# Another order of filter loads and of the first products in a Fourier-mixing and SwiGLU kernel

## The chip, the core and the metric

The kernel runs on one core of a Trainium2 chip. The metric is the time of one execution on the device, in microseconds (us). The core has five engines that run side by side, each through its own list of instructions in order: TensorE (PE) multiplies matrices, VectorE (DVE) and ScalarE (ACT) work element by element and copy results out of PSUM, GpSimd (POOL) works element by element and also starts DMA transfers, and SyncE (SP) only starts transfers. An instruction that waits holds up all that stand behind it on its engine.

## What is computed

The reference takes `x` of shape (8, 3008, 256) and complex filters of shape (1505, 256), given as a real and an imaginary array. It does

```
X = rfft(x, axis=1)
y = irfft(X * (filt_r + i filt_i), n=3008, axis=1)
x2 = y.reshape(24064, 256)
xn = x2 / sqrt(mean(x2^2) + 1e-6) * rms_g
out = (silu(xn @ w_gate) * (xn @ w_val)) @ w_out
```

with `w_gate` and `w_val` of shape (256, 1536) and `w_out` of shape (1536, 256). The output is float32.

## The kernel before

The transform of length 3008 = 64 * 47 is done in two stages of matrix products, with twiddle factors folded into tables. For one batch: stage A multiplies by a 64-point table; a transposition brings the other index onto the partitions; stage B multiplies by a 47-point table for each of 32 indices k (`b_mm`, line 228, two values of k make one unit, so there are 16 units); the result is multiplied by the real and by the imaginary filter (`b_unit`, line 244, the two products L268 and L269); then come the inverse of stage B (`bi_unit`, or `bit_unit` at line 562 for batch 0), another transposition and the inverse of stage A. Then the feed-forward part (`gv`, line 432, and `down`, line 451) goes over 48 blocks of rows, and its products fill PE. The work of batches 1 to 7 is laid out in numbered slots between the blocks of the feed-forward loop; batch 0 has no such loop to lie in, and it comes first, with an order written out by hand (lines 655 to 783). The change touches this part only.

**Batch 0.** `x_load` (line 179) brings the input in four chunks of two transfers each through POOL's queue. `at_unit` (line 525) does stage A. `t1_mm(g)` (line 537) transposes eight 128x128 blocks on PE into PSUM, for four values of k; PSUM has two buffers each for even and odd g. `t1_copy(g, on_act)` (line 555) copies the result out, on ACT (L558) or on DVE (L560). Unit i of stage B needs the copy of g = i // 2. The products of unit i are done by DVE, but for units 3, 7, 9 and 12: there ACT first copies the stage-B result (`v`, L266), and POOL does the two products from that. `inverses` runs `bit_unit` for units of `i`; ACT copies its results (`gT`, L581). `warm_up` issues products of zeros on PE that nothing reads.

**The filters.** Both filter arrays are kept in four groups of eight values of k: tiles `fr0` to `fr3` and `fi0` to `fi3`, of 128 partitions by 8 by 256 float32. `f_load(c, e, eng)` (line 503) loads group c of the real (e = 0) or imaginary (e = 1) array into one half of the partitions, through the queue of `eng`: one transfer of 24 rows of 8 KB (L506) and two of 12 rows in which the eight values of k run backwards (L509, 1 KB pieces); group 0 has a fourth (L513). `f_dup(c, e, eng, lo, hi)` (line 515) copies that half to the other half of the partitions: on ACT (L519), on POOL (L523), or as a transfer on SP's queue (L521). Group c serves units 4c to 4c + 3. Before the loads, the other halves and the gaps are set to zero on DVE (L664), ACT (L652) and POOL (L657, L658).

**The order of loads.** SP's queue carries fr0, fr1, fr2, fr3, fi3 and then the doubling of fr3. POOL's queue carries the input, then fi0, fi1, fi2. A queue's transfers are started in order, and with eight completion semaphores a queue, a transfer is started only when the one eight places before it has landed.

**`gate(ap)`** (line 624) copies one element with POOL into a small tile of its own; it waits for the data it reads, and with it all that stands behind it on POOL. The kernel before defines it and does not call it.

Of the kernel before, what the change touches and what calls it, by code (L numbers as in the profile page):

```python
# [121 lines left out]
def kernel(  # L122
# [11 lines left out]
    nc = tc.nc  # L134

    tab = {k: nc.inline_tensor(np.ascontiguousarray(v), name=k + "_t").ap()
           for k, v in _make_tables().items()}
# [38 lines left out]
    st = {b: {"x": {}, "t1": {}, "t2": {}, "s": {}, "t3": {}, "t4": {}, "y": {}, "sq": {},  # L176
              "u": {}, "xn": {}} for b in range(B)}
# [50 lines left out]
    def b_mm(b, i):  # L228
        ps = bank(3 if b else (0, 3, 4, 5)[i % 4], "psb").rearrange("p (a d) -> p a d", a=2)
        if b == 0 and i > 3:  # L230
            nc.tensor.matmul(ps[:, 0, :], wz[:, 0:P], wz[:, 0:D], start=True, stop=True)
        for u in range(2):
            k = 2 * i + u
            if b:
                w, t = late_p["wb"], st[b]["t2"][k // KC][:, k % KC, :]
            else:
                w, t = wbp, st[0]["t2"][k // 4][:, k % 4, :]
            nc.tensor.matmul(ps[:, u, :], w[:, k, :], t, start=True, stop=True)  # L238
        return ps
# [4 lines left out]
    def b_unit(b, i, ps=None):  # L244
        if ps is None:
            ps = b_mm(b, i)
        f1, f2 = filt(2 * i, 2)
        if b:
            s1 = late_p["sp"].tile([P, 2, D], FP16, tag="s1", name="s1")
            s2 = late_p["sp"].tile([P, 2, D], FP16, tag="s2", name="s2")  # L250
            if summed(b, i):
                nc.vector.tensor_tensor(out=s1, in0=ps, in1=f1, op=ALU.mult)  # L252
                st[b]["s"][i] = (s1, s2, ps, f2)
                return
        elif i % 2:
            s1 = hp.tile([P, 512], FP16, tag="sg", name="sg").rearrange("p (a d) -> p a d", a=2)
            s2 = hhs[(i // 2) % 4].rearrange("p (a d) -> p a d", a=2)
        else:
            ss = xnp.tile([P, 2, 512], FP16, tag="xn", name="ss")
            s1, s2 = (ss[:, e, :].rearrange("p (a d) -> p a d", a=2) for e in range(2))  # L260
        eng = nc.vector
        if (i in (3, 5, 8, 12, 15)) if b else (i in (3, 7, 9, 12)):
            eng = nc.gpsimd
            v = yp.tile([P, 2, 512], FP32, tag="y", name="v")
            v = v[:, 0, :].rearrange("p (a d) -> p a d", a=2)
            nc.scalar.activation(out=v, in_=ps, func=AXT.Copy)  # L266
            ps = v
        eng.tensor_tensor(out=s1, in0=ps, in1=f1, op=ALU.mult)  # L268
        eng.tensor_tensor(out=s2, in0=ps, in1=f2, op=ALU.mult)  # L269
        st[b]["s"][i] = (s1, s2)  # L270
# [229 lines left out]
    def raw(src, row, ap):  # L500
        return bass.AP(tensor=src.tensor, offset=src.offset + row * D, ap=ap)

    def f_load(c, e, eng):
        lo = 1 if c == 0 else 0
        src, t, p0 = ((filt_r, fr[c], 0), (filt_i, fi[c], HALF))[e]
        eng.dma_start(t[p0 + 16:p0 + 63:2, :, :].rearrange("p a d -> p (a d)"),  # L506
                      raw(src, c * KC, [[64 * D, 24], [1, KC * D]]))
        for g in range(2):
            eng.dma_start(t[p0 + 1 + 24 * g:p0 + 24 + 24 * g:2, lo:KC, :],  # L509
                          raw(src, 64 * (1 + 11 * g) - c * KC - lo,  # L510
                              [[64 * D, 12], [-D, KC - lo], [1, D]]))
        if c == 0:
            eng.dma_start(t[p0 + 1:p0 + 48:2, 0, :], raw(src, 32, [[64 * D, 24], [1, D]]))  # L513

    def f_dup(c, e, eng, lo=0, hi=KC):
        t = (fr, fi)[e][c][:, lo:hi, :]
        a, o = (0, HALF) if e else (HALF, 0)
        if eng is nc.scalar:
            eng.activation(out=t[a:a + HALF], in_=t[o:o + HALF], func=AXT.Copy)  # L519
        elif eng is nc.sync:  # L520
            eng.dma_start(t[a:a + HALF], t[o:o + HALF])  # L521
        else:
            eng.tensor_copy(out=t[a:a + HALF], in_=t[o:o + HALF])  # L523
# [13 lines left out]
    def t1_mm(g):  # L537
        if g < 6:
            if g % 2 == 0:
                st[0]["t2t"] = t2p.tile([KR, KC, D], FP16, tag="t2", name="t2")  # L540
            dst = st[0]["t2t"][:, 4 * (g % 2):4 * (g % 2) + 4, :]
        else:
            dst = t3p.tile([KR, 4, D], FP16, tag="t3", name="t2")
        st[0]["t2"][g] = dst
        pool, tag = ((psG, "pg"), (psV, "pv"))[g % 2]
        ps = pool.tile([P, 4, D], FP16, tag=tag, name="pt1")
        af = aT.rearrange("p a k -> p (a k)")
        for a in range(4):
            for dh in range(2):
                b0 = dh * H * P  # L550
                src = af[:, b0:b0 + 32 * P].rearrange("p (i k) -> p k i", k=K2)[:, 4 * g + a, :]
                nc.tensor.transpose(ps[:, a, ts(dh, P)], src, ident)
        st[0]["t2ps"][g] = ps

    def t1_copy(g, on_act):
        dst, ps = st[0]["t2"][g], st[0]["t2ps"].pop(g)
        if on_act:
            nc.scalar.activation(out=dst, in_=ps[0:KR], func=AXT.Copy)  # L558
        else:
            nc.vector.tensor_copy(out=dst, in_=ps[0:KR])  # L560
# [63 lines left out]
    def gate(ap):  # L624

        g = up.tile([1, 1], FP32, tag="gate", name="gate")
        nc.gpsimd.tensor_copy(out=g, in_=ap)
# [8 lines left out]
    with tc.manual_schedule():  # L636
# [28 lines left out]
            zero(fi[c][HALF:P])  # L665
        with nc.allow_non_contiguous_dma(reason="one gain a partition"):
            nc.sync.dma_start(gsb, moe_rms_g.rearrange("(a p) -> p a", p=P))
        for c in range(4):
            f_load(c, 0, nc.sync)
            f_load(c, 1, nc.gpsimd if c < 3 else nc.sync)  # L670

        warm_up(14, 1)
        for g in range(4):
# [14 lines left out]
        def products(*units):  # L688
            for i in units:
                b_unit(0, i, psb.pop(i))  # L690

        def stage_b(*units):
            for i in units:
                psb[i] = b_mm(0, i)

        def inverses(*units):
            for i in units:
                bit_unit(i)

        for g in range(4):  # L700
            t1_mm(g)
            t1_copy(g, g == 1)
        stage_b(0, 1, 2, 3)
        for g in range(4, 8):
            t1_mm(g)
        f_dup(0, 0, A, 0, 2)
        f_dup(0, 1, G, 0, 2)
        f_dup(0, 0, A, 2, 4)
        f_dup(0, 1, G, 2, 8)
        t1_copy(4, 1)  # L710
        f_dup(0, 0, G, 4, 8)
        products(0)
        stage_b(4)
        products(1)
        stage_b(5)
        t1_copy(5, 1)
        f_dup(1, 1, G)
        products(3)
        f_dup(1, 0, A, 0, 4)
        f_dup(1, 0, A, 4, 8)  # L720
        inverses(0, 1)
        products(2)
        t1_copy(6, 0)
        t1_copy(7, 0)
        stage_b(6, 7)
        f_dup(2, 1, G)
        f_dup(3, 0, S)
        products(4, 7)
# [201 lines left out]
```

## Time and profile before

| | |
|---|---|
| median of 6 runs | 886.2 us |
| lowest, highest | 885.66, 888.01 us |
| the profiled execution | 885.66 us, of which the span of the profile is 883.7 us |
| granted TensorE clock | 0.998 |
| busy: PE, DVE, ACT, POOL | 872.9, 678.0, 625.1, 437.6 us |
| first product of the feed-forward loop (L443) | at 45.01 us |
| last inverse product of batch 0 (L573) | at 37.54 us |
| last piece of fi3 copied by ACT (L519) | at 32.83 us |

How to read the rows of a timeline: start in us from the begin of the span, length of the piece in us, engine, line, operation, output<-input, partitions x elements and types, and how many instructions (x2) the row holds; in brackets, how long the engine was idle before it and what ended that. SPq is SP's list of transfers; its rows show when a transfer is started, not when it lands. In the chain of work that ended last, each row is a start, a length and what the end of the program hung on in that time. A row of stretches has start:end, the busy time of each engine with its number of instructions, the granted clock, the DMA engines' mean busy share, and GB/s.

### The profile page before, as it was taken

The numbers are of one execution on the slowest core, as the hardware profiler recorded it, in microseconds if no ns is written. First come the engines' busy times: TensorE is split into PE (matmuls) and PEld (weight loads), VectorE is DVE, ScalarE is ACT, GpSimd is POOL, SyncE is SP. The second block draws the span as 40 slices with busy tenths as digits, with TensorE's granted clock in tenths as the row PEclk, the third lists the DMA queues.
The fourth block names the chain that finished last, engine by engine and source line by source line (L and its number), as shares of the span: only waits on it lengthen the run. The fifth ranks groups of instructions, "written<-read, shape, count | busy, mean of one in ns | idle before, by whom it ended". The sixth has DMA issues, their size and how long they took to land.

```text
span 883.7 us, 17466 instructions
## 1 busy us (share of the span) xinstructions
PE 872.9 (99%) x6257; PEld 559.7 (63%) x6257; DVE 678.0 (77%) x1086; ACT 625.1 (71%) x1070; POOL 437.6 (50%) x394
## 2 busy tenths in 40 slices
PE   9899999999999999999999999999999999999997
PEld 6666666666666666666666666666666666666556
DVE  8866777898878877978687887888778887555555
ACT  8877667677677766876677766887567765676444
POOL 8834831646436752676237661376415761155300
PEclk9999999999999999999999999999999999999999
DMA  9796826665643565434735247322442233222302
GB/s 206 128 186 161 175 70 205 150 142 131 191 122 74 110 144 160 98 96 101 209 83 132 84 100 185 100 80 78 110 141 79 67 84 78 72 64 50 72 24 49
DMA packets 80095, 101.44 MB, mean 115 GB/s; under 512 B 8108, under 2 KB 56684, under 8 KB 79560
## 3 DMA queue, kind: packets, MB, share of 16 engines
q1 hardware_dynamic: 69688, 84.23, 34.5%
q0 software_dynamic: 10240, 15.96, 11.6%
q8 instruction: 49, 0.80, 0.4%
q14 instruction: 38, 0.31, 0.1%
q10 hardware_dynamic: 80, 0.13, 0.1%
HBM read 67.67 MB, written 46.78 MB: 130 GB/s over the span
## 4 chain that ended last, share of the span: by engine, by line
PE 94%; DVE 2%; DMA 2%; ACT 1%; issue 1%; ACTq 0%
PE po L462 28%; PE pg L443 27%; PE pv L443 27%; PE psi L291 3%; PE psb L238 3%; PE psn L323 2%; PE psa L203 2%; DMA fr<-in_filt_r_dram 1%; DMA fi<-in_filt_i_dram 1%; DVE fr L664 1%; PE psq L352 1%; DVE o L472 0%; PE pt L592 0%; ACT gT L581 0%; DVE wi L616 0%
## 5 line engine op out<-in xcount | busy, mean ns | idle before, releaser
L448 DVE TENSOR_TENSOR hh<-pv,sg 128x512 f16<-128x512 f32 (+2 forms) x588 | 392.7, 670 | 189.0 <-ACT sg L447 78.1
L447 ACT ACTIVATE sg<-pg 128x512 f16<-128x512 f32 (+2 forms) x588 | 340.9, 580 | 221.1 <-PE pg L443 211.0
L462 PE MATMUL po<-wo,hh 128*128 128x256 f16 x2244 | 342.2, 272 | 0.7 <-DVE hh L448 0.3
L443 PE MATMUL pv<-xn,wv 128*128 128x512 f16 (+2 forms) x1176 | 339.6, 370 | 0.0
L443 PE MATMUL pg<-xn,wg 128*128 128x512 f16 (+2 forms) x1176 | 339.6, 370 | 0.0
L462 PEld LDWEIGHTS <-hh 128*128 128x128 f16 x2256 | 216.4, 98 | 95.7 <-issue 1.5
L282 POOL TENSOR_TENSOR s<-s,s 128x512 f16<-128x512 f16 x101 | 116.6, 1155 | 223.7 <-DVE s L276 153.9
L443 PEld LDWEIGHTS <-wv 128*128 128x128 f16 x1176 | 114.8, 98 | 128.8 <-issue 0.3
L419 POOL TENSOR_TENSOR xn<-y,rb 128x1024 f16<-128x1024 f32 (+1 forms) x45 | 126.0, 2801 | 54.2 <-DMA rb<-r_tmp 53.1
L443 PEld LDWEIGHTS <-wg 128*128 128x128 f16 x1176 | 111.3, 98 | 13.3 <-issue 0.3
L358 POOL TENSOR_TENSOR rho<-u,mhalf 128x4 f32<-128x4 f32 (+1 forms) x48 | 49.0, 1020 | 61.9 <-DVE u L356 61.7
L296 ACT ACTIVATE t<-psi 96x512 f16<-96x512 f32 x112 | 66.4, 593 | 8.3 <-PE psi L291 3.0
L276 DVE TENSOR_TENSOR s<-psb,fi 64x512 f16<-64x512 f32 x101 | 69.1, 684 | 3.0
L278 DVE SCALAR_TENSOR_TENSOR s<-psb,fi 64x512 f16<-64x512 f32 x101 | 70.0, 693 | 1.4
L329 ACT ACTIVATE y<-psn,gsb 128x512 f32<-128x512 f32 (+1 forms) x94 | 63.8, 679 | 8.1 <-PE psn L323 0.9
L252 DVE TENSOR_TENSOR s<-psb,fr 128x512 f16<-128x512 f32 x101 | 68.8, 681 | 0.0
L343 POOL TENSOR_TENSOR sq<-sq 128x512 f16<-128x512 f16 (+1 forms) x35 | 39.6, 1130 | 36.0 <-ACT sq L335 36.0
L335 ACT ACTIVATE sq<-psn 128x512 f16<-128x512 f32 (+1 forms) x94 | 54.8, 583 | 0.0
L208 ACT ACTIVATE t<-psa 128x512 f16<-128x512 f32 x70 | 41.8, 597 | 5.5 <-PE psa L203 2.4
L291 PE MATMUL psi<-s,wi 128*128 128x256 f16 x238 | 44.3, 273 | 0.0
L238 PE MATMUL psb<-t,wb 96*128 96x256 f16 x224 | 43.0, 272 | 0.3 <-DVE s L269 0.2
L323 PEld LDWEIGHTS <-t 128*128 128x128 f16 x368 | 28.4, 98 | 20.6 <-issue 0.4
(106 smaller groups left out, 526.8 us busy)
## 6 DMA issues: line engine op xcount, KB each, us to landing
out_dram<-o SPq DMA_DIRECT2D x83, 256.0 KB
xc<-in_x_dram POOLq DMA_DIRECT2D x56, 192.0 KB, 6.0
z_tmp<-t SPq DMA_DIRECT2D x28, 384.0 KB
t<-z_tmp SPq DMA_DIRECT2D x28, 384.0 KB
g_tmp<-t SPq DMA_DIRECT2D x56, 192.0 KB
rb<-r_tmp SPq DMA_DIRECT2D x41, 256.0 KB
t<-g_tmp SPq DMA_DIRECT2D x21, 384.0 KB
t<-g_tmp SPq DMA_DIRECT2D x7, 320.0 KB
```

Source lines behind the costliest of these rows:

```text
L238: nc.tensor.matmul(ps[:, u, :], w[:, k, :], t, start=True, stop=True)
L252: nc.vector.tensor_tensor(out=s1, in0=ps, in1=f1, op=ALU.mult)
L276: nc.vector.tensor_tensor(out=s2[a], in0=ps[e], in1=f2[e], op=ALU.mult)
L278: nc.vector.scalar_tensor_tensor(out=s2[a], in0=ps[e], scalar=-1.0, in1=f2[e], op0=ALU.mult, op1=ALU.mult)
L282: nc.gpsimd.tensor_tensor(out=s, in0=s1, in1=s2, op=ALU.add)
L291: nc.tensor.matmul(ps[:, u, :], wi_at(q, 2 * i + u), ss[q][:, u, :], start=(q == 0), stop=(q == n - 1))
L296: nc.scalar.activation(out=st[b]["t3"][c][:, 2 * r:2 * r + 2, :], in_=ps[0:KR], func=AXT.Copy)
L419: nc.gpsimd.tensor_tensor(out=xv, in0=yv, in1=rv.unsqueeze(1).to_broadcast([P, 2, n, P]), op=ALU.mult)
L443: nc.tensor.matmul(ps[:, 0:w], wt[:, dt_, ts(jt, P)], xn[:, dt_, :], start=(dt_ == 0), stop=(dt_ == 1))
L447: nc.scalar.activation(out=sg[:, 0:w], in_=pg[:, 0:w], func=AXT.Silu)
L448: nc.vector.tensor_tensor(out=hh[:, 0:w], in0=pv[:, 0:w], in1=sg[:, 0:w], op=ALU.mult)
L462: nc.tensor.matmul(po[s4 // per][:, s4 % per, :], hh[:, ts(s4, P)], wo[:, jt, :], start=(jt == 0 and s4 % per == 0), stop=(jt == JT - 1 an ...
```

## The change

Two places of the order written out by hand change; no function does.

The loads: fi1 moves from POOL's queue to SP's, between fr0 and fr1. On POOL, a gate on the first half of the last input chunk stands between the loads of fi0 and of fi2. The order on SP's queue becomes fr0, fi1, fr1, fr2, fr3, fi3.

```diff
-        for c in range(4):
-            f_load(c, 0, nc.sync)
-            f_load(c, 1, nc.gpsimd if c < 3 else nc.sync)
+        f_load(0, 0, nc.sync)
+        f_load(0, 1, nc.gpsimd)
+        f_load(1, 1, nc.sync)
+        f_load(1, 0, nc.sync)
+        gate(st[0]["x"][3][0:1, 0, 0:1])
+        f_load(2, 1, nc.gpsimd)
+        f_load(2, 0, nc.sync)
+        f_load(3, 0, nc.sync)
+        f_load(3, 1, nc.sync)
```

The order of work: the transposes of batch 0, which stood in two blocks of four, are spread, and stage B, the products and the copies stand between them. `A`, `G`, `S` are ACT, POOL and SP.

```diff
-        for g in range(4):
-            t1_mm(g)
-            t1_copy(g, g == 1)
-        stage_b(0, 1, 2, 3)
-        for g in range(4, 8):
-            t1_mm(g)
+        t1_mm(0)
+        t1_copy(0, 0)
         f_dup(0, 0, A, 0, 2)
         f_dup(0, 1, G, 0, 2)
+        t1_mm(1)
+        stage_b(0, 1)
         f_dup(0, 0, A, 2, 4)
         f_dup(0, 1, G, 2, 8)
-        t1_copy(4, 1)
+        t1_copy(1, 1)
+        t1_mm(2)
+        t1_mm(3)
         f_dup(0, 0, G, 4, 8)
         products(0)
+        stage_b(2, 3)
+        products(1)
+        t1_copy(2, 0)
+        for g in range(4, 7):
+            t1_mm(g)
         stage_b(4)
-        products(1)
-        stage_b(5)
-        t1_copy(5, 1)
         f_dup(1, 1, G)
         products(3)
+        t1_copy(4, 1)
+        t1_copy(5, 1)
+        products(2)
+        t1_copy(3, 0)
+        t1_mm(7)
+        stage_b(5)
         f_dup(1, 0, A, 0, 4)
         f_dup(1, 0, A, 4, 8)
         inverses(0, 1)
-        products(2)
+        stage_b(6)
         t1_copy(6, 0)
         t1_copy(7, 0)
-        stage_b(6, 7)
+        stage_b(7)
```

What follows (`f_dup(2, 1, G)` and on) is the same in both.

## The prediction

> **What bounds the kernel now.** I read the page's busy table first: PE is busy 872.9 of 883.7 us, and it waits for next to nothing once the feed-forward loop runs (first product L443 at 45.01). Nothing of that loop is touched, so a microsecond won or lost before 45.01 shifts everything behind it by the same amount. So only the start counts. There I read the chain that ended last, in order of time (start, length, what):
>
> ```profile
> 15.60 8.66 DMA fr<-in_filt_r_dram
> 24.28 6.27 DMA fi<-in_filt_i_dram
> 30.61 0.04 issue
> 30.65 0.29 ACT fi L519
> 30.94 0.67 issue
> 31.61 0.57 ACT v L266
> 32.19 0.75 ACT gT L581 x2
> ```
>
> From 15.60 to 30.6 the end is set by SP's filter loads, the last being fi3. Behind it come ACT's copy of fi3 (L519) and ACT's further work. Next SP's own timeline. A load there waits for the load eight places before it (the instruction list shows this: eight completion semaphores in turn), so a start after a wait dates a landing.
>
> ```profile
> 19.61 2.13 SPq L509 DMA_DIRECT2D fr<-in_filt_r_dram  x2
> 21.85 0.77 SPq L506 DMA_DIRECT2D fi<-in_filt_i_dram  x1
> 22.97 2.09 SPq L509 DMA_DIRECT2D fi<-in_filt_i_dram  x2
> 28.64 0.57 SPq L521 DMA_DIRECT2D fr<-fr  x1
> ```
>
> The first row waits for the last part of fr0, which is therefore there by 19.61. The row at 22.97 waits for the last of fr1. The chain's start at 24.28 is fi3's third load, which waits for the first part of fr2. The row at 28.64 waits for all of fr3. So the groups on SP's queue are complete at about 19.6, 22.97, between 24.28 and 27.18 (where ACT copies fr2), 28.6 and 30.6: four groups in 11.0 us, 2.75 each. Then ACT, POOL and DVE from 18 on:
>
> ```profile
> 18.93 1.02 ACT L558 ACTIVATE t<-pt 96x1024 f16<-96x1024 f16 x1 [1.55 <-PE pt L552]
> 19.98 1.17 ACT L519 ACTIVATE fr<-fr 64x512 f32<-64x512 f32 x2
> 21.33 1.93 ACT L558 ACTIVATE t<-pt 96x1024 f16<-96x1024 f16 x2 [0.19 <-PE pt L552]
> 23.16 0.59 ACT L266 ACTIVATE v<-psb 128x512 f32<-128x512 f32 x1
> 23.77 2.00 ACT L519 ACTIVATE fr<-fr 64x1024 f32<-64x1024 f32 x2
> ```
> ```profile
> 18.17 2.04 POOL L523 COPY fi<-fi 64x512 f32<-64x512 f32 x2
> 20.27 1.05 POOL L523 COPY fr<-fr 64x1024 f32<-64x1024 f32 x1
> 21.38 1.92 POOL L523 COPY fi<-fi 64x2048 f32<-64x2048 f32 x1
> 23.90 1.27 POOL L268 TENSOR_TENSOR sg<-v,fr 128x512 f16<-128x512 f32 x1 [0.60 <-ACT v L266]
> ```
> ```profile
> 20.67 0.68 DVE L268 TENSOR_TENSOR ss<-psb,fr 128x512 f16<-128x512 f32 x1
> 25.45 0.67 DVE L268 TENSOR_TENSOR ss<-psb,fr 128x512 f16<-128x512 f32 x1
> ```
>
> All three are almost without a gap from here to 30.6. On ACT each piece starts where the last ended (2.00 at 23.77 ends at 25.77, the next row starts at 25.80). So loads and engines are about equally late: a gain needs both, a loss only one.
>
> **POOL's loads and the gate.** POOL loses fi1's three issues (0.53 + 0.63 + 0.59) and gains the gate, a copy of one element that waits for the first half of the last input chunk. fi1's third load waited for just that input load, eight places before it, until 14.15; so the gate opens at 14.15. The trace has no such tiny copy; its price lies between the 0.10 of a 128x1 memset on POOL (at 0.24) and the 1.04 of the 128x4 power (L358). I take 0.1, the nearer in size. Behind it stand fi2's three issues (0.54 + 1.14) and then fi0's copy: the issues end between 15.9 and 16.9. The copy cannot start before fi0's last load lands, 11.32 + 6.7 = 18.0, so POOL waits there with 1.1 to 2 us in hand and the gate costs nothing; without that cover it would cost its own 0.1 to 1.04. It also holds nothing back: before, fi2 went out at 15.85; now at about 14.3. fi2 then lands near 15.5 + 7.1 = 22.6, wanted at 27.4 below. No gain.
>
> **SP's queue.** fi1 takes fr1's place, fr1 fr2's, fr2 fr3's, fr3 fi3's, and fi3 goes into a sixth place. fi1 was complete at 14.15 + 7.1 = 21.2; now at fr1's 22.97. POOL copies it then, not at 21.38: 22.97 + 1.92 = 24.9, against 23.90 for the product behind it: **+1.0** on POOL, whose later pieces follow without a gap. fi3's sixth place: between 24.4 and 28.4 SP's queue alone moved 0.64 MB, 160 GB/s, so a group of 0.39 MB takes 2.45 us. Against that, POOL's queue is empty some 3 us sooner. With POOL's traffic beside it SP's queue moved 95 GB/s from 15 to 19 and 163 from 21.2 to 24.2, so in those 3 us it wins between 0 and 0.19 MB, 1.2 us. fi3 then lands 1.25 to 2.45 later; outer ends are 0 (the whole load bound by bytes alone) and 2.75 (the mean spacing above). I take **+1.6**, nearer the lower end as both streams together (257 GB/s from 21 to 23) beat either alone: fi3 at 32.2, and fr3, with its doubling on SP's queue behind fi3, as much later. DVE's product 13 at 33.33 stands behind that doubling.
>
> The Trainium skill, "DMA: Bandwidth & Descriptors", section "Issuing engines are not separate DMA queues", says that loads of all issuers run on the same 16 engines and that spreading them saves only issue time. By it the move would cost the loads nothing and the sum would be +1.15 (the order of work alone). The trace disagrees so far as SP's queue alone moves 178 GB/s from 25 to 27, and 257 GB/s moved with both from 21 to 23. The same page, "Why a DMA increments its semaphore by 16 and not by 1", lets a transfer use the largest number of engines up to 16 that divides its rows; for loads of 24 or 12 rows that is 12, which speaks against one queue.
>
> **The order of work.** The number of PE, DVE and ACT instructions is unchanged; only places change. PE issues 0 and 1 of stage B right after two transposes, so DVE's first product no longer waits for two copies, and ACT's copy of fr0 comes first. That copy waits for fr0 until 19.6; done at 20.25, so DVE's product starts at about 20.3, not 20.67: 0.35 won. But ACT's transpose copy 1, which ran from 18.93 to 19.95 in the shadow of that wait, now stands behind it. On ACT: fr0's two halves 19.6 + 1.17 = 20.8; copy 1 to 21.8; stage B of units 2 and 3 on PE (half of the 1.04 for four units) to 22.3; v of unit 3 to 22.9; copies 4 and 5, 1.93, to 24.9. fr1's copy starts there, against 23.77: **+1.15**. Bounds: with fr0 landing at 19.0 instead it is +0.55; if fr1, now third, lands as late as 27.18 it is +3.4; the third place of before has its first part at 24.28, so I take about 25 and no extra wait. On DVE: products 0 and 1 to 22.7, copy 2 to 23.3, product 2 to 24.5, copies 3 and 6 to 25.7. Copy 7 follows a transpose that waits for ACT's copy 5 (24.9 + 0.65 on PE), so it ends at 26.3, and product 4 starts there, against 25.45: +0.9. The 0.35 is lost again, because the same copies now stand between products.
>
> **The sum.** These delays lie side by side, not one behind another: ACT reaches fi3's copy at 30.65 + 1.15 = 31.8, fi3 lands at 32.2, POOL is 1.0 late, DVE 0.9. The latest sets the end: 32.2 - 30.65 = about **+1.6**. Nothing between 31 and 45 makes it up: ACT's gaps there (0.76 and 0.33) are waits for PE's inverse products, themselves fed by ACT. The feed-forward weights leave POOL 1.0 later, from 36.8; the first third of gate and value weights lands by 37.6 + 6.9 = 44.5, ahead of their first use, which moves to 46.6. The profiled run took 885.66, its span plus 2.0, and becomes 887.3. It is the fastest of the six, 0.5 under the median of 886.2, so the median becomes **887.8**.
>
> **Rivals.** (1) The waits add up: the sixth place costs its full 2.75, or fr1 misses ACT's 24.9 and stragglers come on top. For it: a group took 3.4 us from 19.6 to 22.97; against: the later spacing was shorter. +2.75 to +3.9, median 889.0 to 890.1. Chance 0.2. (2) The loads are hidden after all: fi3 lands before 31.8 and only ACT's order counts, +0.55 to +1.15: 886.8 to 887.4. For it: the bytes are the same. Chance 0.2. (3) Faster: with fi1 out of POOL's queue, fr0 lands early and SP's queue alone speeds up. The 2 to 4 us stretch moved 310 GB/s in both queues; if SP's came near it, the 1.2 MB left after 21.5 would be in before 28.5 and the chain loses up to 2.1: 884.1. It decides only if ACT copies fr0 before 18.9 (no copy is held up) and fi3 before 30.65. Against: 160 to 178 GB/s when alone, and a DMA share of 0.79 there already. Chance 0.1. The forecast (+1.2 to +2.3, 887.4 to 888.5) has 0.5.
>
> **How the numbers follow.** 0.2% is 1.8 us, about what a measurement of this kernel can tell from no change. Half of the forecast's case lies over it, as does rival 1; rival 2 and the other half lie within. So slower 0.45, same 0.45, faster 0.1. The range runs from 885.4, under rival 2 by the spread of the runs shown, to 889.6, in the middle of rival 1, and leaves out rival 3 and the rest of 1.
>
> **What would show it.** Right: ACT's fr0 copy at 19.6 with transpose copy 1 behind it; POOL's fi1 copy near 23 after a wait for a load; fr1's copy near 25; fi3's copy near 32; first L443 near 46.6. Wrong: fr0 copied before 18.9, or fi3 copied by 30.7, or a wait for fr1 beyond 25.5.

## The result and the profile after

The kernel after takes 888.94 us (median of 21 runs, 887.01 to 890.62); the kernel before, run beside it, 886.93 us (42 runs, 885.44 to 889.35). The ratio is 1.0022, 95% interval 1.0016 to 1.0028: slower by 1.95 us (1.4 to 2.5). The forecast was +1.6 us. The sign and the size hold; the mechanism that was named as the one setting the end does not.

The profiled execution took 888.47 us, its span 886.6, and the feed-forward loop starts 3.15 us later than in the profile of before:

| | before | after |
|---|---|---|
| profiled execution, us | 885.66 | 888.47 |
| first product of the loop (L443) at | 45.01 | 48.16 |
| execution less that start | 840.65 | 840.31 |
| ACT copies fr0 / fr1 / fi3 at | 19.98 / 23.77 / 30.65 | 20.66 / 26.98 / 33.81 |
| POOL copies fi0 / fi1 at | 18.17 / 21.38 | 19.94 / 24.89 |

The third row is the first finding: what comes behind the start of the loop takes the same in both, so all that is lost is lost ahead of it. In all 14 profiles told of here it is 840.2 to 841.0 us (the execution's time less the loop's start).

The chain of waits of the kernel after (start, length, what):

```profile
10.59 9.44 DMA fr<-in_filt_r_dram
20.05 6.83 DMA fr<-in_filt_r_dram
...
26.98 1.06 ACT fr L519
...
29.09 3.10 DMA fi<-in_filt_i_dram
...
32.42 0.87 ACT gT L581 x2
33.29 0.50 ACT v L266
33.81 1.05 ACT fi L519
```

The chain still goes over the loads, but the waiting is done at another place: up to 26.88 the end hangs on transfers of `fr`, and ACT's copy of fr1 starts straight behind them. Below, fi3's landing at 32.19 stands in the chain too, but ACT does two other pieces before it turns to fi3 at 33.81: fi3 is there 1.6 us before anyone asks for it. ACT's timeline tells it more plainly:

```profile
20.66 1.15 ACT L519 ACTIVATE fr<-fr 64x512 f32<-64x512 f32 x2 [3.28 <-POOL fi L523]
21.84 1.02 ACT L558 ACTIVATE t<-pt 96x1024 f16<-96x1024 f16 x1
23.54 0.60 ACT L266 ACTIVATE v<-psb 128x512 f32<-128x512 f32 x1 [0.68 <-PE psb L238]
24.23 1.93 ACT L558 ACTIVATE t<-pt 96x1024 f16<-96x1024 f16 x2
26.98 2.00 ACT L519 ACTIVATE fr<-fr 64x1024 f32<-64x1024 f32 x2 [0.82 <-DMA fr<-in_filt_r_dram]
```

Three things are to be seen. Transpose copy 1 (21.84) stands behind fr0's copy, as the change wrote it. Copies 4 and 5 end at 26.16, and then ACT is idle until fr1 is there. From 26.98 on ACT works without a gap as far as fi3's copy, 6.83 us later (6.88 before). The releaser of the first row (POOL) is an inference of the profile; ACT's copy needs the load of fr0.

POOL, with the gate and the loads that stand behind it:

```profile
14.18 0.18 POOL L627 CAST gate<-xc 1x1 f32<-1x1 f16 x1 [2.24 <-DMA xc<-in_x_dram]
...
15.22 1.23 POOL L509 DMA_DIRECT2D fi<-in_filt_i_dram  x2
...
19.94 2.02 POOL L523 COPY fi<-fi 64x512 f32<-64x512 f32 x2 [3.50 <-DMA fi<-in_filt_i_dram]
24.89 1.89 POOL L523 COPY fi<-fi 64x2048 f32<-64x2048 f32 x1 [1.84 <-DMA fr<-in_filt_r_dram]
```

The gate takes 0.18 us and opens when it was said to; behind it POOL waits 3.50 us for fi0 anyway. fi1, now second on SP's queue, is copied at 24.89 instead of 21.38. (The last row names a transfer of `fr` as the releaser, again by inference; the copy needs fi1.) And SP, where the last parts of fr1 are started:

```profile
18.59 2.24 SPq L509 DMA_DIRECT2D fr<-in_filt_r_dram  x2
```

They go out from 18.59 on, the second of them at 20.05: the chain above hangs, up to 20.03, on a part of fr0 that was started at 10.59, eight places ahead. ACT has fr1 at 26.9.

### The profile page after: what moved, and what is told of

It reads as the page before. It is cut to its first block, busy times and chain, and to the rows that moved or that the text cites. A ratio compares the mean times of both kernels' runs of the same rounds, so it can differ in the third digit from the quotient of the medians.

```text
span 886.6 us, 17469 instructions
## 1 busy us (share of the span) xinstructions
PE 874.3 (99%) x6257; PEld 561.1 (63%) x6257; DVE 678.1 (76%) x1086; ACT 625.2 (71%) x1070; POOL 436.0 (49%) x392
## 4 chain that ended last, share of the span: by engine, by line
PE 93%; DMA 2%; ACT 1%; DVE 1%; POOL 1%; issue 1%; SPq 0%; ACTq 0%; POOLq 0%
PE po L462 27%; PE pg L443 27%; PE pv L443 27%; PE psi L291 3%; PE psb L238 3%; PE psn L323 2%; PE psa L203 2%; DMA fr<-in_filt_r_dram 2%; PE psq L352 1%; POOL xc L188 0%; DVE o L472 0%; ACT gT L581 0%; PE pt L592 0%; DMA fi<-in_filt_i_dram 0%; DVE hh L448 0%
## 5 line engine op out<-in xcount | busy, mean ns | idle before, releaser
L443 PE MATMUL pv<-xn,wv 128*128 128x512 f16 (+2 forms) x1176 | 339.6, 370 | 0.0
L443 PE MATMUL pg<-xn,wg 128*128 128x512 f16 (+2 forms) x1176 | 339.5, 370 | 0.0
L443 PEld LDWEIGHTS <-wv 128*128 128x128 f16 x1176 | 114.9, 98 | 128.8 <-issue 0.3
L443 PEld LDWEIGHTS <-wg 128*128 128x128 f16 x1176 | 111.3, 98 | 13.4 <-issue 0.3
```

The costliest lines, as they stand in the source:

```text
L443: nc.tensor.matmul(ps[:, 0:w], wt[:, dt_, ts(jt, P)], xn[:, dt_, :], start=(dt_ == 0), stop=(dt_ == 1))
```

## The experiments

Theories. **F**, the forecast: delays lie side by side and fi3's sixth place on SP's queue is the latest. **A**: fr1's third place is; fr1 lands two or three us later than before and everything on ACT behind its copy moves with it. **B**: the order of work is; transpose copy 1 behind fr0's copy holds PE up for some 2 us (and its clock falls), and ACT is late by that alone. Each ratio is to the kernel before, measured beside it; 0.001 is 0.89 us. The intervals reach about 1 us to each side, so that a single part is often not resolved by the time, and the profile must say what happened. Profiles are single executions.

**Each half of the change alone.** New loads in the old order of work, and old loads in the new one:

```diff
 # e1: after, with the order of work of before
-        t1_mm(0)
-        t1_copy(0, 0)
+        for g in range(4):
+            t1_mm(g)
+            t1_copy(g, g == 1)
...
 # e2: after, with the loads of before
-        f_load(1, 1, nc.sync)
...
+        for c in range(4):
+            f_load(c, 0, nc.sync)
+            f_load(c, 1, nc.gpsimd if c < 3 else nc.sync)
```

> The new order of the loads with the old order of work. Forecast's theory (fi3's sixth place sets the end): fi3 lands near 32.2 and its copy on ACT starts there, +1.3 to +1.8 us over the kernel before, nearly all of the change's +2.0. Rival A (fr1's third place: ACT's copy of fr1 waits for it): the copy of fr1 starts at 26 to 27 instead of 23.77 and all behind it is as late, +2 to +3. Rival B (order of work and the half clock it causes on PE): the loads alone cost 0 to 0.5, and PE's clock stays 1.0.

> The old order of the loads with the new order of work. Forecast's theory: ACT's transpose copy 1 stands behind the wait for fr0, +0.55 to +1.15 us. Rival A (fr1 late): fr1 is there by 23, so no wait for it and +0.5 at most. Rival B (PE idles behind copy 1, its clock falls to a half for some 3.5 us): an idle stretch of 2 us or more and a clock of 0.5 behind it, +1.5 to +2.5.

Measured: e1 1.0009 (0.9999 to 1.0019), e2 1.0013 (1.0000 to 1.0026). ACT in e1, then in e2:

```profile
19.98 1.17 ACT L519 ACTIVATE fr<-fr 64x512 f32<-64x512 f32 x2
27.65 2.00 ACT L519 ACTIVATE fr<-fr 64x1024 f32<-64x1024 f32 x2 [3.92 <-DMA fr<-in_filt_r_dram]
```
```profile
20.18 1.16 ACT L519 ACTIVATE fr<-fr 64x512 f32<-64x512 f32 x2 [2.79 <-DMA fr<-in_filt_r_dram]
21.36 1.02 ACT L558 ACTIVATE t<-pt 96x1024 f16<-96x1024 f16 x1
23.57 1.92 ACT L558 ACTIVATE t<-pt 96x1024 f16<-96x1024 f16 x2
25.51 2.01 ACT L519 ACTIVATE fr<-fr 64x1024 f32<-64x1024 f32 x2
```

In time e1 loses 0.8 us (-0.1 to 1.7): that is under A's +2 to +3, and does not decide between F's 1.3 to 1.8 and B's 0 to 0.5. e2 loses 1.2 us (0 to 2.3), which excludes none of the three prices; but PE was idle there for 1.60 us at most and its clock stayed at 1.00, against B. With the loads alone ACT would be free at 23.7, as before, and waits 3.92 us for fr1. With the order alone fr1 is there, and ACT itself comes 5.33 us after its copy of fr0 (3.79 before). So both halves put fr1's copy late, by different ways, and in the kernel after they lie side by side: 26.16 for ACT's work, 26.9 for the load. F has no place for the 3.92.

**Copy 1 back ahead of fr0's copies; PE kept busy.** e3 changes one place of the kernel after; e4 puts 20 products of zeros into the gap in which PE waits for copy 1 (they go into the bank that unit 2 overwrites).

```diff
 # e3
+        t1_copy(1, 1)
         f_dup(0, 0, A, 0, 2)
...
-        t1_copy(1, 1)
 # e4, in b_mm
+        if b == 0 and i == 2:
+            for _ in range(20):
+                nc.tensor.matmul(ps[:, 0, :], wz[:, 0:P], wz[:, 0:D], start=True, stop=True)
```

> The changed kernel with ACT's transpose copy 1 ahead of its copies of fr0, as before. Rival B (copy 1 held up): PE idles less than 1 us, its clock stays 1.0, and 1 us or more of the change's +2.0 is given back. Rival A (fr1's third place): the copy of fr1 starts when fr1 lands, at 26 to 27, whatever comes ahead of it; less than 0.5 given back. Forecast's theory: fi3's landing at 32.2 sets the end; 0.4 given back at most (to +1.6).

> The changed kernel with 20 products of zeros (0.11 us each, 2.1 us) into the result bank of unit 2, ahead of its real products, where PE idled 2.1 us. If the half clock has a price of its own (rival B): clock 1.0 throughout, transposes 4 to 7 faster by 1 us, 0.7 to 1.2 us given back. Rival A: the copy of fr1 still waits for fr1 to land; within 0.3 us of the changed kernel. Forecast's theory: no difference, the clock is off the path.

Measured: e3 1.0003 (0.9992 to 1.0014), e4 1.0005 (0.9995 to 1.0015): by the point values they give back 1.7 and 1.5 us of the 1.95, and their intervals end just below the 1.0016 at which that of the kernel after begins. That is more than F and A allowed (0.5 us at most) and what B asked for in e3 (1 us or more), in e4 even more than it asked for (0.7 to 1.2). The profiles show the way: fr1's copy on ACT starts at 26.27 in e3, still after a gap of 2.57 us, and at 25.91 in e4, without one; the loop starts 21.18 and 21.20 us behind it. In e4 PE's clock stays at 1.00, and the 24 transposes behind unit 3 take 1.67 us against 2.56 at half clock in the kernel after. That the clock is worth what e4 gave back is not shown: fr1 also landed a microsecond sooner there, and fr0 was copied at 19.08 instead of 20.66, which e4's edit, behind that copy, can't have done.

**Both kernels once more.** The landings move from one execution to the next, so each was profiled again, unchanged.

> The kernel before, unchanged, profiled a second time. If landings are steady from run to run (as the forecast took them), fr0 is copied on ACT at 20.0, fr1 at 23.8, fi3 at 30.7 and the first product of the loop starts at 45.0, each within 0.2 us. If one late DMA engine moves them from run to run (the first profile was near the fastest run), they are 0.5 to 2 us later here and the start of the loop lies between 45 and 46.5. The time is the same as before's within its interval.

> The changed kernel, unchanged, profiled a second time beside the others: +1.4 to +2.5 us again. Rival A (fr1's third place): ACT's copy of fr1 starts between 25.5 and 27.7 and in most runs waits for a load. Rival B: PE idles 2 us behind copy 1 and its clock falls to 0.5 again. Forecast's theory: fi3's copy on ACT starts when fi3 lands, near 32.2; in the first profile it started 1.6 us after that.

Measured: 0.9998 (0.9990 to 1.0007) and 1.0019 (1.0010 to 1.0028). In the second profile of before fr1's copy starts at 25.30 and the loop at 47.20, in that of after at 27.27 and 48.45. So the first profile of before, with 23.77 and 45.01, was an early one (it is also the fastest of its six runs), and the 3.15 us between the first two profiles overstate the change. In the second pair fr1's copy moves by 1.97, close to the 1.95 of the times; the loop's start moves by 1.25 only, since that execution of before lost 0.7 more behind fr1's copy (PE ran at a clock of 0.5 there, from 29.4 to 36.2). In the second profile of after ACT waits 0.86 us ahead of fr1's copy, as A said, and F's fi3 is copied at 34.09 without a wait. PE was idle for 1.65 us behind copy 1 and its clock stayed at 1.00, and yet ACT's copy of fr1 and the loop come no sooner than in the first: the half clock of the first profile shows no price here.

**Which load stands third.** e7 has e1's order of work, and fr1 ahead of fi1 on SP's queue; e8 has the loads of before and e3's order.

```diff
 # e7, against e1
-        f_load(1, 1, nc.sync)
         f_load(1, 0, nc.sync)
+        f_load(1, 1, nc.sync)
```

> The old order of work with the new loads, but fr1 in the second and fi1 in the third place of SP's queue. Rival A in its plain form (what waits is whatever stands third): ACT's copy of fr1 no longer waits (near 23.8), POOL's copy of fi1 waits to 26 or 27 and DVE's product 4 and POOL's product 3 with it; +2.5 to +4 us in the profile. Forecast's theory (the sixth place alone): +1.6, the same as with fi1 second.

> The old order of the loads with the new order of work, but ACT's transpose copy 1 ahead of its copies of fr0. If the order's whole loss is copy 1's place, nothing of it is left: within 0.5 us of the kernel before, PE's clock 1.0. As v of unit 3 then stands ahead of copies 4 and 5 on ACT (21.3, not 23.2), POOL's product 3 starts when fi1 is copied, near 23.3, 0.6 earlier than before; if POOL sets the end, 0.5 us faster than before; if ACT or the loads do, the same.

Measured: e7 1.0018 (1.0007 to 1.0029), e8 1.0005 (0.9997 to 1.0014). e7 loses 1.6 us (0.6 to 2.6) in time, F's figure, but not by F's way: ACT copies fr1 at 24.00 and fi3, in the sixth place, at 31.57, neither after a wait, and now POOL waits for what stands third:

```profile
24.99 1.89 POOL L523 COPY fi<-fi 64x2048 f32<-64x2048 f32 x1 [3.23 <-DMA fi<-in_filt_i_dram]
31.57 1.05 ACT L519 ACTIVATE fi<-fi 64x1024 f32<-64x1024 f32 x1
```

The delay has changed its owner and not gone: PE then waits for POOL's products (0.97), ACT for PE (0.96), though PE also ran at a clock of 0.5 by then (28.3 to 35.1), so that POOL's part isn't separated. With either order the group in the third place came too late for its reader. In e8, with copy 1 first again, the time is within 0.5 us of before by the point value. fr1's copy starts at 23.98, too, and there ACT does wait for fi3, by 0.26 us (at 31.68); it is the only one of these profiles in which it does, and fi3 has the fifth place there.

**The sixth place taken away; the gate taken away.** e10 moves fi3's three loads to POOL's queue behind fi2's, so that SP's queue has five groups as before; e9 leaves out the gate; e12 is e10 with copy 1 first; e11 is the kernel before with three zero products instead of one ahead of each unit of stage B beyond the first four.

```diff
 # e9
-        gate(st[0]["x"][3][0:1, 0, 0:1])
 # e10 (e12: the same and e3's edit)
         f_load(2, 1, nc.gpsimd)
+        f_load(3, 1, nc.gpsimd)
...
-        f_load(3, 1, nc.sync)
 # e11, against before, in b_mm
-            nc.tensor.matmul(ps[:, 0, :], wz[:, 0:P], wz[:, 0:D], start=True, stop=True)
+            for _ in range(3):
+                nc.tensor.matmul(ps[:, 0, :], wz[:, 0:P], wz[:, 0:D], start=True, stop=True)
```

> The kernel after without the gate, so fi2's loads go out as soon as POOL has issued fi0's. The forecast's theory (the gate costs 0.1 to 0.2 of POOL's time, under the wait for fi0): 0 +- 0.3 us against the kernel after, POOL's copy of fi0 starts at the landing of fi0 as before, about 18.1 to 19.9, and fr1's and fi3's copies on ACT stay near 27 and 33.8. A rival (the gate keeps fi2 from colliding with the last of the input and with fr0): the input or fr0 land later, ACT copies fr0 0.3 to 1 us later, and the loop starts as much later. Against the kernel before both expect +1.5 to +2.9 us.

> The kernel after with fi3's three loads on POOL's queue behind fi2's, so that SP's queue carries five groups as in the kernel before and there is no sixth place. The forecast's theory (fi3's sixth place, +1.6, sets the end): ACT copies fi3 by about 32 and the loop starts 1 to 1.6 us sooner than with the kernel after. Rival A (fr1's third place sets ACT's order, and ACT finds fi3 already there): ACT still waits for fr1 until 26 to 27, copies fi3 near 33.8 without a wait, and the loop starts within 0.4 us of the kernel after. Rival B (transpose copy 1 behind fr0's copy): the same as A here, since the order of work is unchanged. A cost of its own: two more waits for completions on POOL, which may hold its copy of fi0 up by 0 to 1 us.

> The kernel before with three zero products instead of one ahead of each unit of stage B beyond the first four, so that PE is idle less between the products of batch 0. If the half clock seen at 29 to 34 in one profile of the kernel before costs time, the loop starts 0.3 to 0.8 us sooner than there (47.20) and the ratio falls to 0.9993 or so; if PE's clock costs nothing there because PE waits for ACT and DVE anyhow (the forecast's theory: only loads and ACT's order count), 0 +- 0.3 us, and if the zero products hold PE up, up to 0.6 us more.

> The kernel after with fi3's loads on POOL's queue and with ACT's transpose copy 1 back ahead of fr0's copies. The forecast's theory (loads and order lie side by side, each about +1.2 to +1.6, both now undone but for fi1's second place): +0.3 to +1.0 us against the kernel before, from fi1 on POOL. Rival A (fr1's third place): ACT waits for fr1 until 26 to 27 after a gap of some 2.5 us, copies fi3 near 33, and the time is that of the kernel after with copy 1 first alone, +0.3 to +1.7 us. In the profile the two differ in ACT's wait ahead of fr1's copy: none by the forecast's theory, over 1.5 us by A.

Measured: e9 1.0026 (1.0016 to 1.0035), e10 1.0040 (1.0027 to 1.0053), e11 0.9999 (0.9991 to 1.0008), e12 1.0041 (1.0028 to 1.0054). F asked for e10 to give back up to 1.6 us. It is 1.6 us slower than the kernel after by the point values (the intervals meet at their edges), and A as it was written, no change, missed as well. ACT in e10:

```profile
23.09 1.93 ACT L558 ACTIVATE t<-pt 96x1024 f16<-96x1024 f16 x2
29.42 2.00 ACT L519 ACTIVATE fr<-fr 64x1024 f32<-64x1024 f32 x2 [4.40 <-DMA fr<-in_filt_r_dram]
36.24 1.05 ACT L519 ACTIVATE fi<-fi 64x1024 f32<-64x1024 f32 x1
```

fr1 lands 2.4 us later still, and fi3's copy stands, as ever, 6.82 us behind fr1's. So e10 moves the landing of fr1 too and is no test of the sixth place alone. fr1's own loads are where they were, in third place on SP's queue; what changed is that fi3's transfers go out from POOL at 15.7 to 18.4 and run beside them. What the two queues moved from 19 to 27 us:

| kernel | SP's queue, MB | POOL's queue, MB |
|---|---|---|
| after, first and second | 1.11, 0.94 | 0.29, 0.36 |
| e1, e3, e4, e9 | 0.94, 1.13, 1.09, 1.28 | 0.16, 0.23, 0.25, 0.08 |
| e10, e12 | 0.61, 0.66 | 0.59, 0.67 |

With fi3 on POOL's queue the two share about evenly, and SP's queue, which carries fr1, gets less than in any of the six profiles above them. The Trainium skill, "DMA: Bandwidth & Descriptors", section "Queues, rings and completion order", says that each DMA engine takes turns between the queues that have work for it, a packet at a time. The even shares of e10 and e12 agree with it: a group moved to the other queue did not get out of the way of the one that is wanted first.

e12 is as slow as e10 although copy 1 is first again: ACT's gap ahead of fr1 is 4.96 us instead of 4.40. Where fr1 lands at 28.7 or later the place of copy 1 counts for nothing. Its 3.6 us (2.5 to 4.8) over before lie beyond both prices given for it (1.0 and 1.7 us at most). e9 is as slow as the kernel after: the gate costs nothing and wins nothing that can be measured. e11 is no faster than before, but its interval, 0.8 us to each side, can't tell a price of the half clock from none. No version here beats before.

**All profiles together.** Where the loop starts follows from where ACT starts fr1's copy:

| kernel | fr1's copy at | loop starts at | between |
|---|---|---|---|
| before, first and second | 23.77, 25.30 | 45.01, 47.20 | 21.24, 21.90 |
| after, first and second | 26.98, 27.27 | 48.16, 48.45 | 21.18, 21.18 |
| e1, e2 | 27.65, 25.51 | 48.81, 46.70 | 21.16, 21.19 |
| e3, e4 | 26.27, 25.91 | 47.45, 47.11 | 21.18, 21.20 |
| e7, e8 | 24.00, 23.98 | 47.22, 46.03 | 23.22, 22.05 |
| e9, e10 | 27.03, 29.42 | 48.22, 50.93 | 21.19, 21.51 |
| e11, e12 | 25.75, 28.66 | 46.93, 49.84 | 21.18, 21.18 |

In ten of fourteen it is 21.16 to 21.24 us, over a range of 4.9 us of fr1's copy. That is the path without slack. The four exceptions lose more behind fr1's copy. In e8 ACT waits there 0.64 for PE (at 26.65) and 0.26 for fi3. In e7 it waits 0.42 for fr2, and 0.34 and 0.96 for PE. The second profile of before and e10 ran at half clock from 29.4 to 36.2 and from 32.2 to 39.1. That this made them late is not shown: e12 ran at half clock for as long (30.5 to 37.4) and e1 from 30.1 to 33.6, and both lost nothing.

## Why the prediction was right, and where it was wrong

- **Only the start counts, and nothing makes it up before the loop.** Right: 840.2 to 841.0 us behind the start in every profile.
- **POOL's loads and the gate cost nothing.** Right: 0.18 us for the gate (0.1 taken, 0.1 to 1.04 as bounds), open at 14.18 (14.15), and a wait of 3.50 behind it for fi0; without the gate the time is the same. That fi0 would land at 18.0 was read from one profile; POOL copied it at 18.1 to 20.1 in the others.
- **fi1 in second place, POOL +1.0.** The direction holds, the size was too small: POOL's copy came at 24.89 and, in the second profile, 23.18, against the 22.97 of the forecast. Where fi1 was second it did not set the end: the loop followed ACT's copy of fr1.
- **fi3's sixth place, +1.6, fi3 at 32.2.** The number is exact (32.19) and its part in the sum is wrong: ACT got to fi3 at 33.81. In none of the seven profiles with fi3 in the sixth place (both of after, e1, e3, e4, e7, e9) did ACT wait for it.
- **The order of work.** Right as a mechanism: 5.3 us from fr0's copy to the place where ACT is free for fr1 were worked out, 5.50 and, in e2, 5.33 measured.
- **The step that failed** is the sentence in the order of work that put fr1 at "about 25 and no extra wait". It came from reading the third place of before, whose first part was in by 24.28. The whole group is what ACT needs, and that was in at 26.9 (26.3 to 27.7 in the other profiles with these loads in which ACT waited for it); the upper bound of that very sentence, 27.18, was the better value. The sign of being wrong that the prediction gave itself, a wait for fr1 beyond 25.5, is what came. So "the latest (fi3) sets the end" named the wrong load. This is the second half of rival 1 (fr1 misses ACT's 24.9), at a price of the forecast's own range.
- **A second value was off beside it.** Of the 2.1 us between the 24.9 at which the forecast had ACT start fr1 and the 26.98 measured, the wait for fr1 is 0.82 and the work 0.2; 1.06 is fr0, which ACT copied at 20.66 and not at 19.6. The 19.6 was read from one trace; in the second profile of after fr0 was copied at 21.09. Without any wait for fr1 ACT would have come to fi3 at 33.0 (26.16 + 6.83), still behind its landing at 32.19.
- **Why the total was near all the same.** By luck: 1.6 for the wrong wait and 1.95 for the right one lie close without one following from the other. The sum was made against the earliest execution of before: fr1's copy at 23.77. With 840.6 us behind the loop's start and 21.2 between fr1's copy and that start, the median of 886.93 stands for fr1's copy near 25.1, and the 888.94 of after for 27.1.
- **The rule weighed in the prediction**, that spreading loads over issuers saves issue time only, would have made the loads' part nothing. e1 gives them 0.8 us (-0.1 to 1.7), and that interval includes nothing. e10 and e12 speak against it: with the same bytes in another queue ACT got fr1 at 29.4 and 28.7, against 27.7 at the latest in the six profiles with fi3 on SP's queue and fi1 second. The same engines underneath did not mean the same landing times.
- **What stays open.** How the 1.95 us divide between the two halves (0.8 and 1.2, both with intervals that reach nothing or nearly so); by what e3 and e4 gain as much as they do in time; and why fr1, third, takes until 26.9. That SP starts its last part only at 20.05, when a part of fr0 has landed, isn't the whole reason: in e1 it started at 18.18 and landed later still, at 27.55.

## What to carry to other kernels

When loads change places in a queue, write for each the time at which its first reader is free, and take the landing of the whole group, not of its first part; the load with the least slack sets the end, and it need not be the last one. Moving a transfer to another queue need not take it out of the way of an urgent one: here the urgent one came later. Profile a kernel twice before differences of a microsecond between two traces are read as an effect: here the unchanged kernel's own landmarks moved by 1.5 us.

## What the hardware showed that was not expected

**PE's clock fell after short idle times.** In the kernel after, PE is idle for 2.12 us (to 22.91), and from 23.6 to 27.0 the granted clock is 0.5; e10, idle for 4.11 us up to 31.85, has it from 32.2 to 39.1. The PE row and the stretch from 23 to 27 us of the kernel after:

```profile
22.91 0.60 PE L238 MATMUL psb<-t,wbp 96*128 96x256 f16 x4 [2.12 <-ACT t L558]
```
```profile
23.00:27.00 4.00, 4.00 (x38) 3.78 (x38) 3.79 (x7) 2.56 (x4) 2.07 (x3) 0.58 0.80 188
```

In e9 a gap of 1.92 us was enough, in the second profile of before one of 2.04. In the second profile of after the gap was 1.65 us and the clock stayed at 1.00, but so it did in e8 behind a gap of 1.98: the length of one gap alone does not decide. Read in steps of 0.2 us, the clock was at 0.5 for 3.4 us in the kernel after, e1 and e9, and for 6.8 us, twice that, in the second profile of before, e7, e10 and e12. The Trainium skill, "TensorE: Matmul & The Clock Gate", section "What's actually happening", gives a free-running window of about 3.4 us, and half rate after at least one idle window. The lengths at half rate agree with such a window; the idle times of 1.9 to 2.1 us are shorter than one, so here PE needn't be idle for a whole window.

**The start itself moves by one to two microseconds between executions that load alike.** ACT copied fr0 at 19.98 and 20.89 in the two profiles of before and at 22.02 in e11, where already transpose copy 1, which needs no filter, came at 20.92 instead of 18.93 (PE had waited 1.79 us for the input, up to 17.76). A difference of that size between two traces is no effect of a change by itself.
